# Sliding-window attention and a highway layer: 128-key units in sixteen 32x32 score tiles, v in 512-byte float runs, masks by identity products, a fixed rotation of stages

## The chip, the cores and the metric

The kernel runs on one core of one Trainium2 chip. The metric is the time of one execution on the device in microseconds (us); lower is better. Of the kernel before, three runs gave 235.52, 240.13 and 245.24 us; the median is 240.13. One execution was profiled; the columns and views quoted below are of that one.

The engines are named as in the profile: PE does matrix products (PEld is its loading of the stationary operand), DVE is the vector engine, ACT the scalar engine, POOL the general engine, SP the engine that only issues transfers. DMA queues move data between the chip's main memory and the on-chip memory. Each engine works through its own list of instructions in order, and waits at an instruction until the semaphores that it names are reached.

## The reference

Eight batches, eight heads, 576 positions of 64 numbers each for q, k and v, all float32. Each query sees the 128 keys up to and including its own; a linear penalty by distance, with a slope per head, is added to the scaled scores.

```python
scores = scale * np.matmul(q, k.transpose(0, 1, 3, 2))
rel = pos[:, None] - pos[None, :]
bias = slopes[:, None, None] * (-np.abs(rel).astype(np.float32))[None, :, :]
mask = (rel >= 0) & (rel < window)                # window = 128
scores = np.where(mask, scores + bias[None], -1000000000.0)
attn = softmax(scores)                            # exp, divided by its sum
x = (attn @ v), heads side by side                # 4608 rows of 512
H = np.maximum(x @ w_h, 0.0)
T = 1.0 / (1.0 + np.exp(-(x @ w_t + b_t)))
out = T * H + (1.0 - T) * x
```

So there is an attention part that reads 28 MB of q, k and v, and a highway part with two 512x512 weight matrices for each of 4608 rows.

## The kernel before, in words

The batches are taken two at a time (pair m, 4 of them); r is the batch within a pair. The heads are taken in groups hp of two, hp and hp + 4 (j = 0 and 1), so that one tile of 128 partitions holds 2 batches x 2 heads x 32 groups.

**Loads.** `load` (L103) issues every transfer on POOL's queue, which also turns float32 into bf16 on the way. q and k come as one transfer per pair, hp and tensor (L108), with one run of 18 positions x 64 numbers per partition. v comes as four transfers per pair (L112) straight into its place `VA`, where each partition takes single positions: its runs are 64 numbers, 128 bytes after the conversion. DVE then transposes q and k in 32x32 squares (`tr`, L169), with two bf16 numbers taken as one 32-bit word, so that TR holds a head's numbers along the partitions and its positions along the row.

**Attention.** A unit is (m, s, hp): 128 keys of two batches and two heads. `scores` (L189) multiplies keys by queries on PE with tiles of 32 rows by 64 columns: a quarter of the rows for each (r, j), and the half of the columns that belongs to j. So of the eight squares of 32 rows by 64 columns it uses four. There are 24 products in a unit, each over 192, 128 or 64 queries. ACT takes exp of the result (`soft`, L204) with the penalty's part by key in its bias; DVE multiplies by the window and the rest of the penalty (`mask`, L214). `pv` (L237) multiplies by v with a column of ones appended, in tiles of 64 rows by 128 columns, and `norm` (L249, L251) divides by that column's sum.

**Highway.** For each of 36 blocks of 128 rows: PE transposes x (L260), ACT copies it to the on-chip memory (L265), PE multiplies by w_h (L271) and by w_t (L284), with the bias b_t as a fifth product (L286). ACT takes tanh (L290) and turns it into the gate (L294, 0.5 t + 0.5); DVE does max(., 0) - x (L276) and multiplies by the gate (L298); POOL adds x (L302); SP stores (L309, L313).

**The order of the work** is written by hand in the string ORDER (L15): each letter calls one step (`do`, L315) on the next item of its list in `lists`. What comes from one letter stands in that order on every engine that it touches. The on-chip accumulator memory holds two tiles for scores (`ps_sc`), one for `av` and two `f` tiles that x's transposes and the two products share.

## Time and profile before

| What | Value |
|---|---|
| median of 3 runs | 240.13 us (235.52 to 245.24) |
| profiled execution: its span, first to last instruction (the page gives no other time of it) | 234.4 us |
| PE busy | 148.7 us, 2677 products |
| DVE busy | 141.5 us, 273 instructions |
| ACT busy | 114.4 us, 175 instructions |
| POOL busy | 86.6 us, 95 instructions |
| read from main memory, written to it | 30.41 MB, 9.44 MB |

The page's second part cuts the span into 40 slices of 5.86 us; a digit is the busy share of a slice in tenths. PEclk is the clock that PE was granted, in tenths of full speed. DMA is the mean busy share of the 16 transfer engines, and GB/s what they moved, counted in bytes as written. A row of a list of instructions by line reads: line, engine, operation, output<-inputs, shapes, count | busy time and mean duration in ns of one | idle time before them and what ended it. A row of a timeline reads: start, duration, engine, line, operation, count; several instructions of one form that follow each other are one row. In a timeline the duration of a product runs until its last result is out, so products that follow each other overlap; the start of the next row tells how fast they go in.

### The profile page before, as it was taken

What the parts mean: (1) busy time and instruction counts of PE and PEld (TensorE: products, weight loads), DVE (VectorE), ACT (ScalarE), POOL (GpSimd) and SP (SyncE); (2) the same over time, 40 slices, a digit from 0 to 9 for tenths busy, and PEclk for the clock granted to TensorE, in tenths of its full rate; (3) what the DMA queues carried; (4) which work ended last, traced back from release to release, by engine and by line L of the source; (5) the groups of instructions that cost most, each with busy time, mean ns of one, the idle gap of its engine ahead of it and who ended that gap; (6) DMA issues with size and microseconds to landing.
All of it is one profiled execution on the core that took longest, in us unless ns stands there. A gap on an engine that the chain in (4) does not pass through costs nothing. (4 is left out here: it accounts for less than half of the span.)

```text
span 234.4 us, 6181 instructions
## 1 busy us (share of the span) xinstructions
PE 148.7 (63%) x2677; PEld 88.6 (38%) x2708; DVE 141.5 (60%) x273; ACT 114.4 (49%) x175; POOL 86.6 (37%) x95
## 2 busy tenths in 40 slices
PE   0028122777399303017569869998899999999760
PEld 0017012554244201003236355545556555666320
DVE  2774115885964003010499998999977768796330
ACT  2018100474148600104426765877569589795560
POOL 6192215245411653235924223132233234233331
PEclk9999999999859955555759999999999999999996
DMA  2999999999999999999999941212113221221223
GB/s 25 154 97 74 78 167 184 184 144 135 77 76 133 188 142 71 82 162 207 151 99 218 119 115 48 92 49 78 59 23 116 92 92 65 73 82 60 90 90 91
DMA packets 60380, 25.09 MB, mean 107 GB/s; under 512 B 50625, under 2 KB 51649, under 8 KB 60353
## 3 DMA queue, kind: packets, MB, share of 16 engines
q0 software_dynamic: 55104, 15.26, 153.6%
q1 hardware_dynamic: 5248, 9.44, 12.9%
q8 instruction: 21, 0.34, 0.7%
q14 instruction: 7, 0.05, 0.1%
HBM read 30.41 MB, written 9.44 MB: 170 GB/s over the span
## 5 line engine op out<-in xcount | busy, mean ns | idle before, releaser
L204 ACT ACTIVATE p<-sc,bias 128x768 bf16<-128x768 f32 x64 | 55.7, 907 | 64.5 <-PE sc L189 63.1
L302 POOL TENSOR_TENSOR ot<-uu,x 128x512 f32<-128x512 bf16 x36 | 43.1, 1198 | 75.7 <-DVE uu L298 54.7
L276 DVE SCALAR_TENSOR_TENSOR uu<-f,x 128x512 bf16<-128x512 f32 x36 | 24.6, 685 | 49.4 <-POOL ot L302 40.4
L189 PE MATMUL sc<-tr,tr 32*64 32x192 bf16 (+2 forms) x1152 | 36.6, 267 | 24.7 <-DVE tr L169 16.3
L284 PE MATMUL f<-wT,xt 128*128 128x512 bf16 x128 | 39.9, 413 | 15.2 <-DVE uu L276 12.9
L271 PE MATMUL f<-wH,xt 128*128 128x512 bf16 x129 | 36.3, 390 | 14.8 <-DVE uu L276 13.1
L214 DVE TENSOR_TENSOR p<-p,mk 128x768 bf16<-128x768 bf16 x64 | 37.9, 611 | 9.6 <-ACT p L204 9.6
L290 ACT ACTIVATE tt<-f 128x512 f16<-128x512 f32 x36 | 21.5, 597 | 42.1 <-PE f L286 42.1
L169 DVE STREAM_TRANSPOSE tr<-ld 128x576 uint32<-128x576 uint32 x32 | 39.0, 1243 | 4.2 <-DMA ld<-in_q_dram 4.2
L189 PEld LDWEIGHTS <-tr 32*64 32x64 bf16 x1152 | 27.2, 118 | 29.2 <-DVE tr L169 17.1
L237 PE MATMUL av<-va,p 64*128 64x65 bf16 (+1 forms) x1088 | 26.1, 201 | 19.0 <-DVE x L251 10.7
L237 PEld LDWEIGHTS <-p 64*128 64x128 bf16 (+1 forms) x1088 | 20.9, 102 | 27.5 <-DVE x L251 12.8
L271 PEld LDWEIGHTS <-xt 128*128 128x128 bf16 x144 | 13.0, 99 | 31.9 <-issue 18.9
L251 DVE TENSOR_TENSOR x<-av,rd 128x512 bf16<-128x512 f32 (+1 forms) x32 | 24.3, 758 | 1.2
L284 PEld LDWEIGHTS <-xt 128*128 128x128 bf16 x144 | 13.3, 102 | 30.3 <-issue 19.9
L265 ACT COPY xt<-f 128x512 bf16<-128x512 bf16 x36 | 21.0, 586 | 5.8 <-PE f L260 5.6
L294 ACT ACTIVATE tt<-tt 128x512 f16<-128x512 f16 x36 | 22.9, 636 | 0.6
L112 POOL DMA_DIRECT2D va<-in_v_dram x16 | 18.5, 1168 | 8.5 <-DMA ld<-in_q_dram 8.2
L108 POOL DMA_DIRECT2D ld<-in_q_dram x16 | 11.2, 703 | 24.0 <-DMA va<-in_v_dram 13.2
L298 DVE TENSOR_TENSOR uu<-uu,tt 128x512 bf16<-128x512 bf16 x36 | 15.4, 431 | 7.3 <-ACT tt L294 7.3
L108 POOL DMA_DIRECT2D ld<-in_k_dram x16 | 10.9, 681 | 20.9 <-DMA va<-in_v_dram 14.1
L260 PE MATMUL f<-ident,x 128*128 128x128 bf16 x144 | 14.4, 224 | 4.5 <-DVE uu L276 2.3
(30 smaller groups left out, 46.7 us busy)
## 6 DMA issues: line engine op xcount, KB each, us to landing
out_dram<-ot SPq DMA_DIRECT2D x32, 256.0 KB, 2.0
ld<-in_q_dram POOLq DMA_DIRECT2D x16, 288.0 KB, 19.1
ld<-in_k_dram POOLq DMA_DIRECT2D x16, 288.0 KB, 17.9
va<-in_v_dram POOLq DMA_DIRECT2D x16, 288.0 KB, 17.8
out_dram<-ot SPq DMA_DIRECT2D x8, 128.0 KB, 2.4
wH<-in_moe_w_h_dram POOLq DMA_DIRECT2D x1, 512.0 KB, 20.7
wT<-in_moe_w_t_dram POOLq DMA_DIRECT2D x1, 512.0 KB, 19.1
bT<-in_moe_b_t_dram POOLq DMA_DIRECT2D x1, 1.0 KB, 16.5
```

What stands on the lines that cost most here:

```text
L108: nc.gpsimd.dma_start(out=LD[m % 2, hp, w][:], in_=src)
L169: nc.vector.transpose(out=TR[m % 2, hp, w][:].rearrange("p s e -> p (s e)").bitcast(U32).rearrange("p (s t) -> p t s", t=NT), in_=LD[m % 2 ...
L189: nc.tensor.matmul(out=sc[j * D : (j + 1) * D, r, off : off + n], lhsT=KT[rows, t * D : (t + 1) * D, e], rhs=QT[rows, t * D : t * D + n, e ...
L204: nc.scalar.activation(out=pview(i), in_=SC.pop((m, s, hp))[:, :, 0:384].rearrange("p r (g n) -> p r g n", g=2), func=ACTF.Exp, bias=BIAS[ ...
L214: nc.vector.tensor_tensor(out=p, in0=p, in1=mk.to_broadcast([P, 2, 2, 192]), op=ALU.mult)
L237: nc.tensor.matmul(out=av[orow, j, slot * (D + 1) : (slot + 1) * (D + 1)], lhsT=pt[rows, r, off : off + orow.stop - orow.start], rhs=VA[m] ...
L251: nc.vector.tensor_tensor(out=x[:, :, 0:nt, :], in0=av[:, :, 0:nt, 0:D], in1=rd[:, :, 0:nt, :].to_broadcast([P, 2, nt, D]), op=ALU.mult)
L271: nc.tensor.matmul(out=pa[:], lhsT=XT[m, s, b][:, c, :], rhs=wH[:, c, :], start=c == 0, stop=c == NC - 1)
L276: nc.vector.scalar_tensor_tensor(out=uu[:], in0=PA.pop((m, s, b))[:].rearrange("p (c n) -> p c n", c=NC), scalar=0.0, in1=X[m, s][:, :, b, ...
L284: nc.tensor.matmul(out=pz[:], lhsT=xt[:, c, :], rhs=wT[:, c, :], start=c == 0, stop=False)
L294: nc.scalar.activation(out=tt[:], in_=tt[:], func=ACTF.Copy, bias=0.5, scale=0.5)
L302: nc.gpsimd.tensor_tensor(out=ot[:], in0=UU.pop((m, s, b))[:], in1=X[m, s][:, :, b, :], op=ALU.add)
```

## The change

Every function between the loads and the stores is written anew.

- **Units.** A unit is (b, u): 128 keys of one batch and all eight heads, 40 units in all (the fifth of a batch has 64 keys). The two bits of a head's number of 64 are still taken apart (e), the keys into even and odd positions (t). `scores` uses tiles of 32 rows by 32 columns, all sixteen squares of PE: row quarter j is a head within a half, column quarter kap is 2h + g, with h the half of the heads and g the half of the keys.
- **Masks** are put into the score tile by 16 products per unit of a diagonal (SI, slope / scale) with a table (MT) of minus the distance, or minus a million outside the window. ACT's exp has no bias any more, and DVE's multiplication is gone.
- **v** is loaded by SP's queue as float32 into VS, two positions (512 bytes) to a run, and DVE casts it into VA, four instructions per batch.
- **q and k** come as one transfer per batch and tensor, with the same run length as before; those of the first batch in quarters.
- **Blocks** of 128 rows begin at position 64; the first 64 rows of two batches make one block. `pv` takes 16 products of 64 rows by 128 columns and up to 32 of 32 rows by 64 columns per block. The bias b_t comes as 16 products of 32 rows by 64 columns, put between those.
- **Highway.** The gate's 0.5 t + 0.5 goes from ACT to DVE; the multiplication by the gate goes from DVE to POOL, but for the last two blocks.
- **Order.** ORDER and `lists` are gone. A loop over the 36 blocks issues in each round: the scores of the next block's unit, the product with v of this block, the highway products of the block before, and the transposes of x of this block; the transposes and casts for the next batch and the loads are dealt out in fixed numbers per round. The score tile has one buffer of four banks.

The core of the diff:

```diff
-ORDER = (
-    "LLLLSLLTLTLseTLmLTLsLseLesmLesmLesmLesmLesmLeLmLmLLLLpLnLTpLnTpLsnLeLTpmLTLnsLseLesmLpem"
...
-    return by
+NB, NU, NJ = 8, 5, 4
...
+    LD = {(i, w): cp.tile([P, 2, NT * D], BF16, name=f"ld{i}{w}")
+          for i in range(3) for w in range(2)}
+
+    TR = {(i, w, h): cp.tile([P, S, 2], BF16, name=f"tr{i}{w}{h}")
+          for i in range(2) for w in range(2) for h in range(2)}
+
+    VS = [cp.tile([P, NJ, NU, 2 * D], F32, name=f"vs{i}") for i in range(3)]
+    VA = [cp.tile([P, NJ, NU, 2, D + 1], BF16, name=f"va{i}") for i in range(4)]
+
+    PR = [cp.tile([P, NJ, 384], BF16, name=f"pr{i}") for i in range(6)]
+    PS = [cp.tile([P, NJ, 384], BF16, name=f"ps{i}") for i in range(2)]
...
+    def load_v(b, half, j):
+        rows = 64 * half
+        if j == NJ:
+            nc.sync.dma_start(
+                out=VS[b % 3][rows : rows + 32, :, 4, :],
+                in_=v[b, 4 * half : 4 * half + 4, 512:576].rearrange(
+                    "j (p t) d -> p j (t d)", t=2))
         else:
-            if at[0] < 2:
-                nc.gpsimd.dma_start(
-                    out=(wH, wT)[at[0]][:],
-                    in_=(moe_w_h, moe_w_t)[at[0]].rearrange("(c p) n -> p c n", p=P))
-            else:
-                nc.gpsimd.dma_start(
-                    out=bT[0:1, :], in_=moe_b_t.rearrange("(o n) -> o n", o=1))
+            nc.sync.dma_start(
+                out=VS[b % 3][rows : rows + 64, j, 0:4, :],
+                in_=v[b, 4 * half + j, 0:512].rearrange("(u p t) d -> p u (t d)", p=64, t=2))
+
+    def cast_v(b, j):
+        nc.vector.tensor_copy(
+            out=VA[b % 4][:, j, :, :, 0:D],
+            in_=VS[b % 3][:, j].rearrange("p u (t d) -> p u t d", t=2))
...
+    def scores(b, u):
+        sc = SC[b, u] = ps_sc.tile([P, NJ, 512], F32, name="sc")
+        for h in range(2):
+            for g in range(2):
+                for j in range(NJ):
+                    rows, kap = slice(32 * j, 32 * j + 32), 2 * h + g
+                    o = sc[32 * kap : 32 * kap + 32, j, 0:384]
+                    m = MT[rows, g].rearrange("p t c n -> p (t c n)")
+                    if u == 4:
+                        o = o.rearrange("p (t n) -> p t n", t=2)[:, :, 0:D]
+                        m = MT[rows, g, :, 0, :]
+                    nc.tensor.matmul(out=o, lhsT=SI[rows, h, :], rhs=m, start=True,
+                                     stop=u == 4 and g == 1, tile_position=(32 * j, 32 * kap))
+        parts = [(0, 128 * u, 0, 192 if u < 4 else 64)]
+        if u < 4:
+            parts.append((1, 128 * u + 64, 64, 128))
+        if u < 3:
+            parts.append((1, 128 * u + 192, 0, 64))
+        for t in range(2):
+            for e in range(2):
+                for g, qs, off, n in parts:
+                    for h in range(2):
+                        for j in range(NJ):
+                            rows, kap = slice(32 * j, 32 * j + 32), 2 * h + g
+                            k0 = 128 * u + 64 * g + t
+                            nc.tensor.matmul(
+                                out=sc[32 * kap : 32 * kap + 32, j, 192 * t + off : 192 * t + off + n],
+                                lhsT=TR[b % 2, 1, h][rows, k0 : k0 + 63 : 2, e],
+                                rhs=TR[b % 2, 0, h][rows, qs : qs + n, e],
+                                start=False,
+                                stop=t == 1 and e == 1 and (g, off) in ((0, 0), (1, 0 if u < 3 else 64)),
+                                tile_position=(32 * j, 32 * kap))
...
-    def mask(m, s, hp):
-        p = pview(PT[m, s, hp])
-        mk = MK[:, hp : hp + 1, :].rearrange("p o (g n) -> p o g n", g=2)
-        if s < 3:
-            mk = mk[:, :, 0:1, :]
-        nc.vector.tensor_tensor(out=p, in0=p, in1=mk.to_broadcast([P, 2, 2, 192]), op=ALU.mult)
...
+        nc.scalar.activation(out=o, in_=i, func=ACTF.Exp, scale=scale)
...
+            if tau:
+                for j in range(NJ):
+                    for t in range(2):
+                        for h in range(2):
+                            one_mm(b, tau - 1, slice(64 * h, 64 * h + 64), h, j, t, D, P,
+                                   slice(0, P))
+            ends = []
+            if tau:
+                ends.append((b, tau, 0, D))
+                if tau > 1:
+                    ends.append((b, tau - 2, 1, 0))
+            else:
+                ends += [(b - 1, 0, 0, 0), (b, 0, 0, D)]
+            for j in range(NJ):
+                for t in range(2):
+                    for h in range(2):
+                        for bb, u, g, o in ends:
+                            r = 64 * h + 32 * g
+                            calls.append((bb, u, slice(r, r + 32), h, j, t, 0, D,
+                                          slice(o, o + D)))
+        if zblk is not None:
+            pz = PZ[zblk] = ps_f.tile([P, DM], F32, name="f")
+        for n in range(8):
+            if blk is not None:
+                w = len(calls) // 8
+                for c in calls[n * w : (n + 1) * w]:
+                    one_mm(*c)
+            if zblk is not None:
+                for i in range(2):
+                    nc.tensor.matmul(
+                        out=pz[i * D : (i + 1) * D, n * D : (n + 1) * D],
+                        lhsT=one[32 * i : 32 * i + 32, :],
+                        rhs=bB[32 * i : 32 * i + 32, n * D : (n + 1) * D],
+                        start=n == 0, stop=False, tile_position=(32 * i, i * D))
+
...
+    def to_gate(blk):
+        nc.vector.tensor_scalar(out=TT[blk][:], in0=TT[blk][:], scalar1=0.5, scalar2=0.5,
+                                op0=ALU.mult, op1=ALU.add)
+
+    def gate(blk, eng):
+        eng.tensor_tensor(out=UU[blk][:], in0=UU[blk][:], in1=TT.pop(blk)[:], op=ALU.mult)
+
+    def add_x(blk, eng):
+        ot = OT[blk] = ft.tile([P, DM], F32, name="ot")
+        eng.tensor_tensor(out=ot[:], in0=UU.pop(blk)[:], in1=X.pop(blk)[:], op=ALU.add)
...
-            nc.tensor.matmul(out=pz[:], lhsT=xt[:, c, :], rhs=wT[:, c, :],
-                             start=c == 0, stop=False)
-        nc.tensor.matmul(out=pz[:], lhsT=ones0[:], rhs=bT[:], start=False, stop=True)
...
-    def to_gate(m, s, b):
-        tt = TT[m, s, b]
-        nc.scalar.activation(out=tt[:], in_=tt[:], func=ACTF.Copy, bias=0.5, scale=0.5)
-    def gate(m, s, b):
-        uu = UU[m, s, b][:].rearrange("p c n -> p (c n)")
-        nc.vector.tensor_tensor(out=uu, in0=uu, in1=TT.pop((m, s, b))[:], op=ALU.mult)
-
-    def add_x(m, s, b):
-        ot = OT[m, s, b] = ft.tile([P, NC, P], F32, name="ot")
-        nc.gpsimd.tensor_tensor(out=ot[:], in0=UU.pop((m, s, b))[:], in1=X[m, s][:, :, b, :],
-                                op=ALU.add)
...
-        for n, step in enumerate("".join(ORDER)):
-            if step == "S":
...
-                continue
-            do[step](*by[step][at[step]])
-            at[step] += 1
...
+        load_b(0)
+        load_b(1)
...
+        for part in range(2):
+            for h in range(2):
+                for w in range(2):
+                    tr(0, w, h, part, True)
+                    if part == 0 and h == 0 and w == 0:
+                        v_clear(0)
+                        issue(vloads, 10)
+            if part == 0:
+                scores(0, 0)
+                soft(0, 0)
+        for b in range(1, 3):
+            v_clear(b)
...
+        cst(4, 0)
+        nc.vector.memset(wT[:, :, 0:1], 0.0)
+        load_w(1)
+        load_w(0)
+        scores(0, 1)
+        soft(0, 1)
+        issue(loads, 4)
+        issue(vloads, 10)
...
+        for p in range(N + 1):
+            blk = blocks[p] if p < N else None
+            nxt = blocks[p + 1] if p + 1 < N else None
+            if nxt is not None:
+                scores(*nxt)
+                soft(*nxt)
+            pv(blk, prev)
+
+            tb = -1
+            if blk is not None:
+                tb = blk[0] + (2 if blk[1] == 4 else 1)
+                norm(blk)
+            if p > 2:
+                trn(2 if blk and blk[0] % 2 == 0 and blk[1] in (1, 2) else 1, tb)
+            if prev is not None:
+                mm_z(prev)
+                tanh(prev)
+                to_gate(prev)
+            if nxt is not None and nxt[0] % 2 and nxt[1] == 4 and nxt[0] + 1 < NB:
+                trn(8, nxt[0] + 1)
+                scores(nxt[0] + 1, 0)
+                soft(nxt[0] + 1, 0)
+            if prev is not None:
+                mm_h(prev)
+                relu_sub(prev)
+            if p > 2:
+                trn(1, tb)
+            cst(1, tb)
+            if blk is not None:
+                x_tr(blk)
+                x_copy(blk)
+            if p == 2:
+                trn(8, tb)
+            if prev is not None:
+                last = p >= N - 1
+                gate(prev, nc.vector if last else nc.gpsimd)
+                add_x(prev, nc.vector if last else nc.gpsimd)
+                store(prev)
+            due = max(0, 10 - 2 * (p + 3) * 2 // 9)
+            issue(loads, len(loads) - due if len(loads) > due else 0)
+            due = max(0, 60 - 10 * (p + 3) * 2 // 9)
+            issue(vloads, len(vloads) - due if len(vloads) > due else 0)
+            prev = blk
+        assert not loads and not vloads and not trs and not casts, (loads, vloads, trs, casts)
 
```

The loop moves instructions on every engine. On DVE, in the steady part of the program, names with numbers as the order lists them, a stretch of two units of the kernel before:

```order
L249 RECIPROCAL rd_2335<-av_2291 128x2x4
L251 TENSOR_TENSOR x_2232<-av_2291,rd_2335 128x2x256
L214 TENSOR_TENSOR p5_120<-p5_120,mk_132 128x4x192
L214 TENSOR_TENSOR p6_121<-p6_121,mk_132 128x4x192
L169 STREAM_TRANSPOSE tr130_109<-ld130_93 128x18x32
L169 STREAM_TRANSPOSE tr131_110<-ld131_94 128x18x32
L298 TENSOR_TENSOR uu_2271<-uu_2271,tt_2345 128x512
L214 TENSOR_TENSOR p7_122<-p7_122,mk_132 128x4x192
L276 SCALAR_TENSOR_TENSOR uu_2443<-f_2409,x_1887 128x512
```

and one round of the changed kernel (L280 and L281 divide, L165 transposes q and k, L318 makes the gate, L314 does max(., 0) - x, L101 casts v):

```order
L280 RECIPROCAL rd_3319<-av_3268 128x8
L281 TENSOR_TENSOR x_3318<-av_3268,rd_3319 128x512
L165 STREAM_TRANSPOSE tr001_86<-ld10_81 128x9x32
L318 TENSOR_SCALAR tt_3327<-tt_3327 128x512
L314 SCALAR_TENSOR_TENSOR uu_3335<-f_3330,x_3119 128x512
L165 STREAM_TRANSPOSE tr001_86<-ld10_81 128x9x32
L101 CAST va0_96<-vs1_94 128x10x64
```

The masks (L214) and the multiplication by the gate (L298) are gone from DVE; the gate itself, a cast and two transposes of half the size stand in every round, with the first transpose between the division and the gate.

On POOL, at the start of the program, the kernel before has these transfers behind the first four:

```order
L164 AFFINE_SELECT ident_130<-ident_130 128x128
L112 DMA va0_111<-in_v_dram 64x36x64 x4
L108 DMA ld020_83<-in_q_dram 128x1x1152
L108 DMA ld021_84<-in_k_dram 128x1x1152
L108 DMA ld030_85<-in_q_dram 128x1x1152
L108 DMA ld031_86<-in_k_dram 128x1x1152
L117 DMA wH_127<-in_moe_w_h_dram 128x4x512
L117 DMA wT_128<-in_moe_w_t_dram 128x4x512
```

and the changed kernel these, from the last quarter of the first batch's q and k on:

```order
L83 DMA ld01_80<-in_k_dram 128x1x576
L110 DMA bB_110<-in_moe_b_t_dram 1x16x32 x2
L106 DMA wT_109<-in_moe_w_t_dram 128x4x512
L106 DMA wH_108<-in_moe_w_h_dram 128x4x512
L79 DMA ld10_81<-in_q_dram 128x2x1152
L79 DMA ld11_82<-in_k_dram 128x2x1152
L79 DMA ld20_83<-in_q_dram 128x2x1152
L79 DMA ld21_84<-in_k_dram 128x2x1152
L79 DMA ld00_79<-in_q_dram 128x2x1152
L322 TENSOR_TENSOR uu_762<-uu_762,tt_754 128x512
L326 TENSOR_TENSOR ot_773<-uu_762,x_579 128x512
```

The transfers of v have left POOL's queue; the weights stand before q and k of the second batch, and a write to wT by DVE, behind the four casts of the first batch, must come before the load of wT. On POOL two additions or multiplications per block stand where one stood.

374 lines of the change are left out of this document (174 added, 200 removed).

## Prediction

> **What bounds the kernel now.** First the page's slices, to see whether one thing limits the whole span:
>
> ```profile
> PE   0028122777399303017569869998899999999760
> DVE  2774115885964003010499998999977768796330
> PEclk9999999999859955555759999999999999999996
> DMA  2999999999999999999999941212113221221223
> ```
>
> There are two stages. Up to slice 23 (23 x 5.86 = 135 us) the transfer engines are full and PE mostly idles; then the transfers are nearly idle and PE and DVE are full. The windows give the same in sums (columns: stretch, its length, then busy time and count of PE, PEld, DVE, ACT, POOL; PEclk, DMA share, GB/s):
>
> ```profile
> 0.00:30.00 30.00, 7.25 (x153) 5.50 (x154) 14.45 (x53) 8.46 (x11) 13.27 (x23) 1.00 2.80 86
> 30.00:54.00 24.00, 11.44 (x326) 9.23 (x326) 14.22 (x23) 6.96 (x9) 9.16 (x12) 1.00 1.21 173
> 84.00:110.00 26.00, 7.01 (x29) 2.41 (x30) 2.98 (x6) 2.70 (x4) 9.07 (x12) 0.50 3.32 126
> 136.00:180.00 44.00, 39.28 (x834) 24.24 (x844) 40.06 (x70) 31.53 (x51) 12.73 (x11) 1.00 0.22 74
> 12.00:30.00 18.00, 7.25 (x153) 5.50 (x154) 8.20 (x12) 6.88 (x8) 8.24 (x10) 1.00 4.25 84
> ```
>
> From 12 to 30 us nearly only v is on its way, at 84 GB/s; from 30 to 54 us q, k and the weights, at 173. By bytes, then:
>
> ```profile
> ld<-in_q_dram POOLq DMA_DIRECT2D x16, 288.0 KB, 19.1
> ld<-in_k_dram POOLq DMA_DIRECT2D x16, 288.0 KB, 17.9
> va<-in_v_dram POOLq DMA_DIRECT2D x16, 288.0 KB, 17.8
> wH<-in_moe_w_h_dram POOLq DMA_DIRECT2D x1, 512.0 KB, 20.7
> q0 software_dynamic: 55104, 15.26, 153.6%
> q1 hardware_dynamic: 5248, 9.44, 12.9%
> q8 instruction: 21, 0.34, 0.7%
> ```
>
> q and k are 9.4 MB: 55 us; v is 4.7 MB: 56 us; two weights 6 us. That is 117 us for the first stage. v, a third of the bytes, takes half of it. The second stage has PE at 39.28 of 44 us and DVE at 40.06. So the kernel is 135 us of transfers with some 65 us of PE's work beside them, then some 90 us of PE and DVE, then the tail.
>
> **The change: transfers.** v's runs go from 128 to 512 bytes as written, and their number is halved. No transfer of that form stands in the trace. If a run costs what it did, v takes 28 us; if a byte read costs what it did, 56. I take 40 (5 us per batch), between the ends, since nothing here is nearer to one of them. With q, k and the weights that is 101 us, and the stores add q1's 12.9% of 234.4, 30 us: 131 us, to be spread over the whole span. Transfers stop being the bound, unless they come late at the start.
>
> **PE.** The rows that price it, from the timeline:
>
> ```profile
> 141.63 1.03 PE L284 MATMUL f<-wT,xt 128*128 128x512 bf16 x4
> 142.50 0.38 PE L286 MATMUL f<-bT,ones 128*128 128x512 bf16 x1
> 144.92 0.39 PE L260 MATMUL f<-ident,x 128*128 128x128 bf16 x4
> 145.23 0.87 PE L189 MATMUL sc<-tr,tr 32*64 32x192 bf16 x32
> 146.04 1.09 PE L237 MATMUL av<-va,p 64*128 64x65 bf16 x56
> L237 PE MATMUL av<-va,p 64*128 64x65 bf16 x896 | 22.7, 200 | 19.0 <-DVE x L251 10.7 <-DMA va<-in_v_dram 8.1
> ```
>
> Four products of 512 columns go in during 0.87 us: 2,354 columns per us. The 32 score products have 6,144 columns, 2.61 us one by one; they took 0.87 less the 0.20 that a short product is on its way, so 3.9 ran at once. Four is the number of row quarters, and also of the squares that this layout uses. The 56 products with v took (1.09 - 0.20) / 56 = 16 ns each, two at once.
>
> *Scores* of a full unit: 16 mask products of 384 columns and 96 of 192, 128 and 64. Every one of the sixteen squares gets 384 + 768 = 1,152 columns, 0.49 us if all run at once; with 0.20 on the way and 0.1 to change the tile shape (the transposes should have been in after 0.22, the next row starts after 0.31) 0.79. If only four run at once, as the row has it, 18,432 columns take 2.0 and with the rest 2.3. The fifth unit of a batch has a third: 0.46 or 0.97. Over 32 full and 8 short units and 36 blocks: 0.80 or 2.3 per block. I take 0.80: what ran at once in the row were distinct squares, and they lost nothing by sharing an accumulator bank two by two.
>
> The Trainium skill, "TensorE: Matmul & The Clock Gate", Part 3 on packing small matmuls, reports sixteen 32x32 tiles at 10.6 times the rate of one; by that figure a full unit would take 18,432 / 2,354 / 10.6 + 0.3 = 1.04 us, an estimate 0.25 above mine. No run here shows sixteen yet.
>
> *Products with v*: 16 of the old form, 0.25; 32 small ones and 16 for the bias use single row quarters, 8 ns each if four run at once, 16 if two: 0.38 to 0.76; with 0.3 for way and shape 0.93 to 1.3. I take 1.0, near the row with four at once. *Highway*: 8 x 0.2175 = 1.74; the fifth product is gone. *Transposes of x*: 0.31, as before. Sum per block 0.80 + 1.0 + 1.74 + 0.31 = **3.85 us**.
>
> PE's instructions grow from 5,418 to 12,514, and q8 brings them: 0.7% of 16 x 234.4 is 26 us of one engine's time for 0.34 MB, so 61 us for the new count. That is under a third of the span; I cost it at nothing.
>
> **DVE.**
>
> ```profile
> 161.00 0.41 DVE L298 TENSOR_TENSOR uu<-uu,tt 128x512 bf16<-128x512 bf16 x1
> 161.34 1.25 DVE L169 STREAM_TRANSPOSE tr<-ld 128x576 uint32<-128x576 uint32 x1
> 164.19 2.33 DVE L169 STREAM_TRANSPOSE tr<-ld 128x576 uint32<-128x576 uint32 x2
> 166.37 0.41 DVE L298 TENSOR_TENSOR uu<-uu,tt 128x512 bf16<-128x512 bf16 x1
> 167.16 0.68 DVE L276 SCALAR_TENSOR_TENSOR uu<-f,x 128x512 bf16<-128x512 f32 x1
> 167.76 0.19 DVE L249 RECIPROCAL rd<-av 128x8 f32<-128x8 f32 x1
> 167.98 0.69 DVE L251 TENSOR_TENSOR x<-av,rd 128x512 bf16<-128x512 f32 x1
> 168.59 0.55 DVE L214 TENSOR_TENSOR p<-p,mk 128x768 bf16<-128x768 bf16 x1
> L146 DVE TENSOR_SCALAR mk<-qq,kk 128x512 bf16<-128x512 f32 x1 | 0.5, 480 | 0.0
> L146 DVE TENSOR_SCALAR mk<-qq,kk 128x256 bf16<-128x256 f32 x1 | 0.3, 347 | 0.0
> L214 DVE TENSOR_TENSOR p<-p,mk x64: 530/550/1514, 15.4 to 212.9; 128x768 bf16<-128x768 bf16 x64
> ```
>
> From start to start: division 0.83, max(., 0) - x 0.60. A transpose is 2.18 / 2, its half 0.55; of 64 halves 48 fall on the 33 rounds from the fourth on: 0.80. A cast of 640 numbers isn't in the trace; the two L146 rows (float32 in, bf16 out) give 0.52 ns per number, so 0.55, at twice that slope 0.88; 25 in 33 rounds: 0.42. The gate with one input: nearest is L298 with two, 0.34. Sum **3.0 us**, 0.85 below PE. The masks that go, 64 x 0.55 = 35 us, were beside transfers in one half and on DVE's share of the bound in the other.
>
> **ACT and POOL.**
>
> ```profile
> L204 ACT ACTIVATE p<-sc,bias 128x768 bf16<-128x768 f32 x64 | 55.7, 907 | 64.5 <-PE sc L189 63.1
> L290 ACT ACTIVATE tt<-f 128x512 f16<-128x512 f32 x36 | 21.5, 597 | 42.1 <-PE f L286 42.1
> L265 ACT COPY xt<-f 128x512 bf16<-128x512 bf16 x36 | 21.0, 586 | 5.8 <-PE f L260 5.6
> L302 POOL TENSOR_TENSOR ot<-uu,x x36: 1149/1155/1497, 89.7 to 228.9; 128x512 f32<-128x512 bf16 x36
> ```
>
> Exp over 1,536 numbers: 907 + 768 x (907 - 597) / 256 = 1.84 us at most; (32 x 1.84 + 8 x 0.6) / 36 + 0.60 + 0.59 = 2.95 per round. POOL 2 x 1.155 = 2.3. Both lie beside PE. The one score buffer holds up nothing: exp ends 1.9 us after the scores, and PE has 3.0 of other work between two units.
>
> **The round.** PE issues the scores of the next block, the products with v, w_t, w_h, the transposes of x. The division is done 1 us after the products with v, PE needs it after 1.74; tanh (0.60, after exp) frees its buffer while w_h runs. So PE's own 3.85 sets the round, plus its waits: in 136 to 180 us it was busy 0.89 of the time with DVE as full as itself; with DVE at 3.0 I take 0.92, **4.2 us**.
>
> **The start.**
>
> ```profile
> 1.33 0.89 POOL L108 DMA_DIRECT2D ld<-in_q_dram  x1 [0.81 <-POOLq L340]
> 11.02 3.54 DVE L169 STREAM_TRANSPOSE tr<-ld 128x576 uint32<-128x576 uint32 x3 [0.55 <-DMA ld<-in_q_dram]
> ```
>
> Four loads of 295 kB (1.18 MB, 6.8 us at 173 GB/s) were there at 11.0, so 4.2 us are fixed. The four quarters are half of that: 7.6 us, behind which DVE's tables end near 9.5 (an estimate: the first POOL operation that they need comes behind four issues, as before, and the sixteen operations are of L146's size or less); eight half transposes until 14.5. The loads of v start near 10.7, behind a DVE write, and land near 17; four casts until 19. Only then may wT, wH, q and k of the second batch start: 6 + 6.8 us and 2 us of the third batch's v beside them, so k lands near 34 to 35, and six of its eight half transposes are done at **38**. Until then there is work for three rounds only. From there 33 rounds of 4.2 are 139 us; 1 us for the three rounds with a second unit.
>
> PE idles a few us before 38; from 84 to 110 us, where it was idle three quarters of the time, the granted clock was 0.50, so the first rounds may be slower by a us or two. That is left to the range.
>
> **The tail**: bias and the two products 0.3 + 2 x 0.87 + 0.2 = 2.2, max(., 0) - x 0.7, gate and addition on DVE 1.1, then store and end:
>
> ```profile
> out_dram<-ot SPq DMA_DIRECT2D x32, 256.0 KB, 2.0
> ```
>
> With that landing and the 1 us that the end of a program takes, together 7. Span 38 + 139 + 1 + 7 = **185** against 234.4. The median of the runs is 5.7 above the profiled span; with the same, **191 us**.
>
> **Rivals.**
>
> *Four squares at once.* If a row quarter takes one product at a time, the scores cost 2.3, the small products with v 1.3: 5.65 per block, 6.1 per round with the same waits. 38 + 33 x 6.1 + 8 + 5.7 = 253, slower. It turns to slower (245) at a round of 5.85, which is scores of 2.0 with the small products at 1.3. For it: 3.9 at once in the only row. Against: that layout had only four squares to use.
>
> *DVE and POOL shut each other out.* L214's longest is 1,514 against 530, and L302's 1,497 against 1,149: some pairs met. POOL now has 2.3 us in every round. If every gate and cast on DVE waits out a POOL operation (0.96 each, 1.76 per round), DVE needs 4.7 and the round is 5.1: 38 + 168 + 8 + 5.7 = 220. The Trainium skill, "SBUF — State Buffer", section "Who interferes with whom", says that single-input copies and tensor_scalar in their fast modes and POOL's operations lock each other out for a whole instruction; by that rule the two new DVE operations are the exposed kind, and the long L214 fits it. Against: the gate comes when POOL should be done with the block before.
>
> *v isn't relieved.* Runs cost by bytes: 7 us per batch, and the start, which needs three batches of v beside q and k, ends near 45: 198. The change then doesn't do what it says for v, and still gains, since the first stage is no longer PE's idle time.
>
> **How the numbers follow.** Forecast 0.60 (175 to 208: round 3.85 to 4.6, start 34 to 42). v not relieved 0.12. DVE and POOL 0.12. Four squares 0.10. The rest, 0.06, is several in part, 230 to 245. Range 174 to 230. A measurement of this kernel can tell about 2% from no change. Faster by more: 0.60 + 0.12 + 0.11 + 0.01 = 0.84; within: 0.07; slower: the four squares mostly, 0.09.
>
> **What would show it.** Right: DMA's digits below 9 after some 40 us; PE's at 9 from there to the end, PEclk at full; score rows of some 112 products in under 0.9 us; rounds of 4.2 us; the first products with w_t before 28 us. Wrong: score rows of 2 us or more (four squares); DVE casts or gates above 1 us, with DVE at 9 and PE waiting for division (shut out); DMA at 9 beyond 60 us (v); PE waiting for "issue" in the middle of a row of small products (the supply of instructions).

## The result and the profile after

Five runs of the changed kernel gave 244.67 to 250.32 us, median 247.26; five of the kernel before gave a median of 238.78. Executions of one kernel differ by some per cent, and the ratios here and below compare only those within 1.5% of each kernel's fastest, so they differ a little from the quotients of the medians. The ratio is 1.033, with a 95% interval of 1.023 to 1.044: the change makes the kernel slower, where 191 us was forecast. The profiled execution took 249.96 us, a little over the median; its span is 248.1 us.

The page of the changed kernel, its slices (6.2 us each) and queues:

```profile
PE   0245575667956789588946599766958698596982
DVE  2974127544962389265951269535846299332463
PEclk9999999575979799767997569977988799889998
DMA  3996999991488216972587204991252211202222
q0 software_dynamic: 9152, 10.50, 26.6%
q1 hardware_dynamic: 24960, 18.88, 25.7%
q8 instruction: 49, 0.80, 1.3%
```

The transfers did most of what was forecast. They keep the engines nearly full for nine slices (56 us, where some 40 were forecast) instead of 23, and what remains comes in bursts. But PE, which should have been at 9 from the 40th us on, swings between 4 and 9, and its clock, which was full from the 123rd us to the last slice of the kernel before, dips again and again. q8, which brings the instructions, grew from 21 pieces to 49: 12,514 / 49 and, before, 5,418 / 21 both are about 256 instructions to a piece, and 0.80 MB / 49 is 16 KB.

PE's timeline shows both kinds of round. First one without a stall, from one transposing of x to the next, then the stretch from 157 to 170 us (columns: start, duration, line, operation, count; in brackets the idle time ahead of the row and what ended it), and at the end a row at reduced clock and the first and last transposes of the rounds from the fourth on:

```profile
174.30 0.40 PE L288 MATMUL f<-ident,x 128*128 128x128 bf16 x4
174.63 0.38 PE L184 MATMUL sc<-mt,si 32*32 32x384 bf16 x16
174.80 1.08 PE L198 MATMUL sc<-tr,tr 32*32 32x192 bf16 x96
175.81 0.57 PE L233 MATMUL av<-va,pr 64*128 64x65 bf16 x18
...
176.77 0.81 PE L298 MATMUL f<-wT,xt 128*128 128x512 bf16 x3 [0.16 <-issue]
177.42 1.03 PE L309 MATMUL f<-wH,xt 128*128 128x512 bf16 x4
178.32 0.38 PE L288 MATMUL f<-ident,x 128*128 128x128 bf16 x4
...
157.79 0.28 PE L198 MATMUL sc<-tr,tr 32*32 32x192 bf16 x11
158.77 1.03 PE L198 MATMUL sc<-tr,tr 32*32 32x128 bf16 x85 [0.70 <-issue]
...
163.32 0.18 PE L233 MATMUL av<-va,pr 32*64 32x65 bf16 x1 [2.89 <-issue]
...
170.07 0.30 PE L198 MATMUL sc<-tr,tr 32*32 32x192 bf16 x17 [1.66 <-issue]
...
142.96 1.91 PE L309 MATMUL f<-wH,xt 128*128 128x512 bf16 x4
...
51.05 0.58 PE L288 MATMUL f<-ident,x 128*128 128x128 bf16 x4
239.93 0.38 PE L288 MATMUL f<-ident,x 128*128 128x128 bf16 x4
```

The undisturbed round takes 178.32 - 174.30 = 4.02 us, under the 4.2 that were forecast. But the 32 rounds between the last two rows take 188.88 us, 5.90 each. The difference begins in the middle of rows of small products: 11 score products go in, then PE has nothing for 0.70 us; among the products with v it has nothing for 2.89 us; in the next scores for 1.66 us. No engine and no transfer of data is named, only "issue". A window from the one gap to the next tells how many instructions lie between (columns: stretch, length, busy time and count of PE, PEld, DVE, ACT, POOL; PEclk, DMA share, GB/s); the first two rows are a stretch with stalls at half clock and the undisturbed one behind it:

```profile
133.00:147.00 14.00, 10.44 (x335) 6.16 (x323) 4.52 (x8) 4.77 (x6) 3.46 (x4) 0.51 0.25 67
147.00:158.00 11.00, 10.33 (x362) 6.51 (x360) 10.47 (x21) 6.48 (x9) 6.85 (x6) 1.00 0.50 115
158.60:163.20 4.60, 1.66 (x128) 1.42 (x128) 0.00 (x0) 1.45 (x1) 2.82 (x3) 1.00 0.94 248
163.20:169.90 6.70, 4.92 (x127) 2.63 (x128) 4.10 (x7) 1.18 (x2) 2.22 (x2) 0.75 0.65 134
```

128 products and 128 loads of weights, then 127 and 128 (a record can be missing): PE stops once in every 256 instructions, which is one piece of its list. So it goes on: from the 45th us the trace has 17 stalls of over 0.6 us that end in "issue", and from each to the next lie 127 or 128 products, or a whole multiple of that. The trace also has the packets of q8. In all 17 stalls a piece had landed 1.2 to 1.5 us before PE went on; for the three above it landed at 157.37, 161.98 and 168.57 us. PE's longest waits from the 45th to the 240th us, by sums, and the many short ones ahead of w_t, which stand in undisturbed rounds too (columns: total us, times, longest):

```profile
PE av L233 <- issue: 14.6, 7, 3.0
PE sc L198 <- issue: 13.5, 8, 2.8
PE f L270 <- issue: 3.4, 2, 2.0
PE sc L184 <- issue: 3.0, 1, 3.0
PE f L298 <- issue: 6.6, 32, 0.3
```

The first four are 34.5 us. Against rounds that are all as short as the undisturbed one, the excess is 32 x (5.90 - 4.02) = 60 us. Most of the other 26 us go with the clock, which is 0.51 from 133 to 147 us: four products with w_h take 1.91 us there and 1.03 at full clock. By the trace's record of the clock PE was busy for 45.8 us of the 32 rounds at half clock; at that ratio this is some 21 us more than at full clock, an estimate.

The theory, then: PE's list arrives in pieces of 256 instructions, and the next piece isn't there in time when PE has run through the last one too fast. The rivals: the pieces are late only because they queue behind data on the transfer engines; or, third, the small products are slow for some reason of their own.

### The profile page after: what moved, and what is told of

It reads as the page before. It is cut to its first block, busy times and chain, and to the rows that moved or that the text cites. A ratio compares the mean times of both kernels' runs of the same rounds, so it can differ in the third digit from the quotient of the medians.

```text
span 248.1 us, 13351 instructions
## 1 busy us (share of the span) xinstructions
PE 172.5 (70%) x6218; PEld 108.9 (44%) x6256; DVE 136.8 (55%) x271; ACT 94.6 (38%) x113; POOL 101.7 (41%) x104
## 3 DMA queue, kind: packets, MB, share of 16 engines
q1 hardware_dynamic: 24960, 18.88, 25.7%
## 4 chain that ended last, share of the span: by engine, by line
PE 57%; issue 19%; DVE 10%; DMA 9%; ACT 3%; POOL 2%; SPq 0%; POOLq 0%; ACTq 0%; DVEq 0%
PE f L298 13%; PE f L309 13%; PE sc L198 11%; PE av L233 10%; DMA wH<-in_moe_w_h_dram 5%; PE sc L184 4%; DMA vs<-in_v_dram 4%; DVE tr L165 3%; PE f L288 3%; PE f L270 2%; DVE va L101 2%; DVE uu L314 1%; ACT ps L217 1%; POOL ld L83 1%; ACT tt L303 1%
## 5 line engine op out<-in xcount | busy, mean ns | idle before, releaser
L322 POOL TENSOR_TENSOR uu<-uu,tt 128x512 bf16<-128x512 bf16 x34 | 40.2, 1183 | 122.4 <-DVE uu L314 122.4
L217 ACT ACTIVATE pr<-sc 128x1536 bf16<-128x1536 f32 (+1 forms) x36 | 45.4, 1261 | 43.4 <-PE sc L198 43.3
L198 PE MATMUL sc<-tr,tr 32*32 32x128 bf16 (+2 forms) x3072 | 42.3, 247 | 22.4 <-issue 15.1
L198 PEld LDWEIGHTS <-tr 32*32 32x32 bf16 x3072 | 35.1, 103 | 27.5 <-issue 14.1
L233 PE MATMUL av<-va,pr 32*64 32x65 bf16 (+1 forms) x1344 | 34.4, 212 | 14.0 <-issue 13.8
L165 DVE STREAM_TRANSPOSE tr<-ld 128x288 uint32<-128x288 uint32 x64 | 42.6, 700 | 1.4 <-DMA ld<-in_q_dram 0.7
L298 PE MATMUL f<-wT,xt 128*128 128x512 bf16 x109 | 37.4, 460 | 7.4 <-issue 7.0
L280 DVE RECIPROCAL rd<-av 128x8 f32<-128x8 f32 x36 | 7.3, 203 | 62.9 <-PE av L233 62.9
L314 DVE SCALAR_TENSOR_TENSOR uu<-f,x 128x512 bf16<-128x512 f32 x36 | 24.8, 688 | 16.3 <-PE f L309 16.2
L233 PEld LDWEIGHTS <-pr 32*64 32x64 bf16 (+1 forms) x1344 | 26.5, 113 | 13.8 <-issue 10.1
L101 DVE CAST va<-vs 128x640 bf16<-128x640 f32 x32 | 29.3, 917 | 1.3 <-DMA vs<-in_v_dram 1.3
L270 PE MATMUL f<-bB,one 32*64 32x64 bf16 x576 | 21.9, 210 | 6.8 <-issue 6.0
L281 DVE TENSOR_TENSOR x<-av,rd 128x512 bf16<-128x512 f32 x36 | 24.9, 691 | 1.2
L318 DVE TENSOR_SCALAR tt<-tt 128x512 f16<-128x512 f16 x36 | 10.6, 296 | 19.8 <-ACT tt L303 19.3
```

Source lines behind the costliest of these rows:

```text
L101: nc.vector.tensor_copy(out=VA[b % 4][:, j, :, :, 0:D], in_=VS[b % 3][:, j].rearrange("p u (t d) -> p u t d", t=2))
L165: nc.vector.transpose(out=o, in_=ld[:, h, part * 9 * D : (part + 1) * 9 * D].bitcast(U32).rearrange("p (t i) -> p t i", i=32))
L198: nc.tensor.matmul(out=sc[32 * kap : 32 * kap + 32, j, 192 * t + off : 192 * t + off + n], lhsT=TR[b % 2, 1, h][rows, k0 : k0 + 63 : 2, e] ...
L217: nc.scalar.activation(out=o, in_=i, func=ACTF.Exp, scale=scale)
L233: nc.tensor.matmul(out=av[orow, h, 65 * j : 65 * j + 65], lhsT=PT[bb, u][rows, j, 192 * t + off : 192 * t + off + m], rhs=VA[bb % 4][rows, ...
L270: nc.tensor.matmul(out=pz[i * D : (i + 1) * D, n * D : (n + 1) * D], lhsT=one[32 * i : 32 * i + 32, :], rhs=bB[32 * i : 32 * i + 32, n * D ...
```

## The experiments

### The supply by itself

The edit is a kernel of PE's alone; its core:

```diff
+    def small(n, a):
+        for i in range(n):
+            j, kap = i % 4, i // 4 % 4
+            nc.tensor.matmul(
+                out=a[32 * kap : 32 * kap + 32, j, 0:64], lhsT=ld[32 * j : 32 * j + 32, 0:32],
+                rhs=ld[32 * j : 32 * j + 32, 64:128], start=True, stop=True,
...
+        small(2048, acc[0])
...
+        large(1024, 64, acc[1])
...
+        large(512, 128, acc[0])
...
+        large(512, 192, acc[1])
...
+        small(2048, acc[0])
...
```

> What it is: TensorE alone, five stages one after the other, with nothing else in the first four: 2048 small products (32 rows, 32 columns of weights, 64 columns streamed, the sixteen squares in turn), 1024 products of 128x128 by 64 columns, 512 of 128x128 by 128 columns, 512 by 192 columns, and the 2048 small ones again, this time while SyncE's queue loads v in 512-byte runs. It leaves all of the reference's computation out and stores a constant. Theory 1 (TensorE's instruction list comes in pieces of 256 and a piece takes 2.6 to 3.7 us to come, whatever else is moved): 2048 products and their weight loads are 4096 instructions, 16 pieces, so both stages of small products take 42 to 60 us, with a stall at every 256th instruction, and the one with transfers is no more than a fifth longer; of the large ones, only the products of 64 columns are near the supply's pace. Theory 2 (a piece is late only behind the data on the transfer engines): the first stage of small products runs at the squares' own pace, 2048 of them in under 20 us, with no stall at the 256th instruction, and the last one takes 40 us or more.

Its timeline, three rows of the first stage and two of the last, where v is loaded beside it:

```profile
9.34 1.27 PE L50 MATMUL acc<-ld 32*32 32x64 bf16 x128 [2.04 <-issue]
13.07 1.27 PE L50 MATMUL acc<-ld 32*32 32x64 bf16 x128 [2.46 <-issue]
16.53 1.27 PE L50 MATMUL acc<-ld 32*32 32x64 bf16 x128 [2.19 <-issue]
...
192.69 1.40 PE L50 MATMUL acc<-ld 32*32 32x64 bf16 x128 [2.73 <-issue]
196.42 1.39 PE L50 MATMUL acc<-ld 32*32 32x64 bf16 x128 [2.33 <-issue]
```

and the same kernel's groups by form, for the large products (busy time, mean ns of one, idle time):

```profile
L57 PE MATMUL acc<-ld 128*128 128x64 bf16 x1024 | 31.8, 197 | 0.0
```

The theory of the supply holds in its purest form. With nothing on any other engine and the transfer engines idle, 128 products run in 1.27 us, and then PE stands still for 2.0 to 2.7 us, every time. From piece to piece it is 3.73 and 3.46 us in these rows (13.07 - 9.34, 16.53 - 13.07), and 3.45 to 4.00 over the stage, 3.59 on average. The packets of q8 in the trace show what this time consists of. The transfer of the next piece begins 1.0 to 1.5 us after PE has started on a piece, takes 0.9 to 1.4 us, and PE starts on it 1.2 to 1.5 us after it has landed. With v's transfers beside it, which keep the engines two to three tenths busy, a piece takes 3.67 on average, though the granted clock is 0.5 there: traffic of that size changes little. Products of 128x128 by 64 columns, 31.8 us for 8 pieces of 256 instructions, need 3.97 us a piece and never wait. So a piece of 256 instructions that keeps PE for less than some 3.6 us is paid as 3.6 us.

### v for three batches alone

```diff
-        vloads = [(load_v, b, h, j) for b in range(NB) for j in (4, 0, 1, 2, 3) for h in range(2)]
+        vloads = [(load_v, b, h, j) for b in range(3) for j in (4, 0, 1, 2, 3) for h in range(2)]
...
-            due = max(0, 60 - 10 * (p + 3) * 2 // 9)
+            due = max(0, 10 - 10 * (p + 3) * 2 // 9)
```

> What it is: the changed kernel with v loaded for batches 0 to 2 alone; the casts of the later batches read those again, so v of batches 3 to 7 is left out, and 5.9 of its 9.4 MB in 512-byte runs. TensorE's instructions are the same 12,514. Theory 1 (supply of the list by itself): the stalls at every 256th instruction stay, some 20 of them after 50 us, and the time falls by less than 8 us (over 239 us). Theory 2 (the list is late behind v's 512-byte runs on the transfer engines): the stalls go with the traffic after batch 2's loads, and the time falls towards 200 us.

241.28 us, 6 us less than the changed kernel, and a ratio to the kernel before of 1.029 (1.016 to 1.043). Its slices and a queue from the page, and its waits from the 45th to the 240th us:

```profile
DMA  2996999991367111771177101871121111202222
q1 hardware_dynamic: 12640, 12.98, 17.3%
```

```profile
PE av L233 <- issue: 16.9, 8, 3.4
PE sc L198 <- issue: 14.2, 10, 3.4
```

Half of q1's packets are gone and the stalls are all there. The rival of the traffic falls for this kernel.

### Fewer instructions for the same work

Three kernels take instructions away and leave the columns that PE streams nearly as they are. `wide` makes the second half of a unit's scores one product of 192 columns; `fewer_a` also makes the bias one product of 512 columns; `fewer_b` also makes the masks four products of 64 rows by 128 columns:

```diff
-            parts.append((1, 128 * u + 64, 64, 128))
-        if u < 3:
-            parts.append((1, 128 * u + 192, 0, 64))
+            parts.append((1, 128 * u + 64, 64, 192 if u < 3 else 128))
...
+        nc.tensor.matmul(out=pz[:], lhsT=one[:], rhs=bB[:], start=False, stop=True)
...
-                    nc.tensor.matmul(out=o, lhsT=SI[rows, h, :], rhs=m, start=True,
-                                     stop=u == 4 and g == 1, tile_position=(32 * j, 32 * kap))
+            nc.tensor.matmul(out=o, lhsT=SI[rows, j // 2, :], rhs=m, start=True, stop=False,
+                             skip_group_check=True, tile_position=(64 * (j % 2), 0))
```

> What it is: the changed kernel with only the scores' second half as one product of 192 columns: 10,978 instructions, between the change (12,514, 247 us) and the run with 9,898 (213.5 us). Theory 1: the time follows the number of instructions: (12,514 - 10,978) / (12,514 - 9,898) = 0.59 of the way, 224 to 232 us, unless the bias products, which stand inside the second burst, weigh more than their number.

> What it is: the changed kernel with the same computation in 9,898 instead of 12,514 TensorE instructions: the second half of a unit's scores as one product of 192 columns where the change has one of 128 and one of 64 (so the score tile is 4 x 512 and the exp runs over 2048 instead of 1536 elements), and the bias as one product of 512 columns at the end of z. v's transfers, the 32x32 squares and the masks stay. Columns streamed hardly change. Theory 1 (supply): 21% fewer pieces, so at about 3.6 us a piece at the worst the stalls fall from some 37 us to under 15 and the half clock behind them shortens: 200 to 222 us. Theory 2 (v's traffic): as many bytes in as long runs, so the stalls stay: 240 us or more. Theory 3 (32x32 products are slow by themselves): 240 us or more too, with rounds of the same length.

> What it is: the kernel of the run before (one product of 192 columns, one bias product) with the masks as four products of 64 rows by 128 columns of weights and 512 columns a unit instead of sixteen of 32x32: 8,938 TensorE instructions. The masks' own work is about the same where sixteen squares run at once. Theory 1 (supply): the stalls nearly vanish, 195 to 215 us, below the run before by 3 to 12 us. Theory 2 and theory 3: 240 us or more, as the run before.

| Kernel | PE instructions | Median, us | Kernel before beside it | PE's "issue" waits in scores and products with v, 45th us on |
|---|---|---|---|---|
| changed | 12,514 | 247.26 | 238.78 | 28.1 us, 15 times |
| wide | 10,978 | 225.67 | 239.29 | 17.6 us, 9 times |
| fewer_a | 9,898 | 213.54 | 237.50 | 10.6 us, 8 times |
| fewer_b | 8,938 | 210.79 | 237.50 | 8.6 us, 6 times |

The waits of `fewer_b` from the 45th to the 240th us, and its clock by slices of 5.2 us from the page:

```profile
PE av L228 <- issue: 5.0, 3, 2.4
PE sc L193 <- issue: 3.6, 3, 1.7
```

```profile
PEclk9999999966999799999999999978999999999998
```

The first 1,536 instructions, 6.0 pieces, bring 21.6 us: 3.6 us a piece. That is as much as a piece takes in the supply alone, but the clock rose too (0.91 from the 43rd to the 220th us of `wide`, 0.84 from the 43rd to the 240th of the changed kernel), so the agreement may be luck. The next 4.2 pieces bring 12.1 us, 2.9 each; the last 3.75 only 2.75 us, a little under the 3 to 12 expected: a round of `fewer_b` has about as many instructions as a piece and hardly waits any more. The clock dips in six slices only. `fewer_a` has a ratio of 0.910 (0.892 to 0.927) to the kernel before, `fewer_b` 0.899 (0.887 to 0.912), and the slowest run of the two, 216.84 us, is well under the fastest of the kernel before beside them, 232.85: **the change with fewer instructions beats both kernels.** The squares, v's transfers and the casts are the same in `fewer_a`, and most of what fell is time in which PE has nothing: 46 us from the 43rd to the 240th us of the changed kernel, 22 from the 43rd to the 205th of `fewer_a`. So the third theory falls too.

### The kernel before, with more instructions

```diff
-            for e in range(2):
+            for e, n0 in [(e, n0) for n0 in range(0, n, 64) for e in range(2)]:
...
+                        for c in range(n0, n0 + 64, 64):
+                            nc.tensor.matmul(
+                                out=sc[j * D : (j + 1) * D, r, off + c : off + c + 64],
```

> What it is: the kernel before with nothing of the change, but with each of its score products cut into pieces of 64 columns: the same columns, the same results, 9,258 TensorE instructions instead of 5,418. Theory 1 (the supply of instructions): in the first stage, where TensorE waits for transfers, nothing; in the second, where TensorE sets the time, a unit's scores and products with v bring more than 256 instructions in 2 us, so stalls appear at every 256th, and the kernel before gets 8 to 30 us slower (246 to 268 against 238). Rival (the loss belongs to what is particular to the change, the sixteen squares, the masks as products or the casts): within 2% of the kernel before.

252.52 us (248.18 to 256.89) against 239.29 (234.30 to 244.24): 13 us slower, within the 8 to 30 of the supply theory, but not for the reason it gave. Where it expected nothing, in the stage of the transfers, most of the stalls stand. PE's timeline of this kernel at three of them:

```profile
29.44 1.07 PE L190 MATMUL sc<-tr,tr 32*64 32x64 bf16 x65 [8.59 <-issue]
...
68.09 0.43 PE L190 MATMUL sc<-tr,tr 32*64 32x64 bf16 x17 [7.66 <-issue]
...
134.23 0.31 PE L190 MATMUL sc<-tr,tr 32*64 32x64 bf16 x5 [5.20 <-issue]
```

Its waits over the whole span, then from the 136th us on:

```profile
PE sc L190 <- issue: 40.5, 12, 8.6
...
PE sc L190 <- issue: 3.0, 4, 1.1
```

37.5 of 40.5 us lie before the 136th us, where the transfer engines are full; they are eight stalls of 0.7 to 8.6 us. Where one stall follows another by one piece there, the transfer of the next piece begins 3.7 to 7.4 us after PE has started on the one ahead, by the packets of q8, against 1.0 to 1.5 in the supply alone. So the rival of the traffic, which fell for the changed kernel, is right for a stage whose transfer engines are full. And those stalls weren't hidden, as I had thought: it seems that they put off PE's work of the first stage into the second. How much of the 13 us is theirs isn't shown, since PE is also busy for 155.1 us here and for 148.7 in the kernel before.

The kernel before itself had at least two such stalls, and its timeline has them:

```profile
54.06 0.18 PE L189 MATMUL sc<-tr,tr 32*64 32x64 bf16 x1 [2.97 <-issue]
...
64.47 0.85 PE L189 MATMUL sc<-tr,tr 32*64 32x192 bf16 x14 [3.12 <-issue]
```

3 us in the middle of a row of scores, with nothing named, and 1.6 to 1.7 us before each end a packet of q8 had landed: that PE can wait for a piece could have been read there, and its size from q8's row.

### The same instructions in another order

In the changed kernel (`spread`) and in `fewer_b` (`fewer_c`) the products with w_h are put between the scores and the products with v, so that large ones part the two bursts of small ones:

```diff
+            if prev is not None:
+                mm_h(prev)
+                relu_sub(prev)
             pv(blk, prev)
...
-            if prev is not None:
-                mm_h(prev)
-                relu_sub(prev)
```

> What it is: the changed kernel with the same 12,514 instructions in another order: the four products with w_h of the block before stand between the scores and the products with v, instead of behind w_t. So 0.9 us of large products parts the two bursts of small ones. Theory 1a (a steady pace: 256 instructions per some 3.6 us, whatever their order): a round of 376 instructions needs 5.3 us in any order, so at best 42 + 33 x 5.3 + 8 = 225, and what is gained is under the 22 us between that and 247. Theory 1b (only the burst counts, the supply has enough in hand for a round if the burst is parted): the stalls go, under 215 us. Theory 1a is the one I hold: 230 to 248 us.

> What it is: the fastest version so far (8,938 instructions) with the products with w_h moved between the scores and the products with v. Some 9 us of stalls are left in that version after the 45th us, and its clock is below 0.7 in 3 of 40 slices. Theory 1: a round of some 260 instructions takes 4.3 us, more than the 3.6 of a piece, so parting the bursts takes most of the stalls away: 200 to 210 us. If the supply is no longer its limit: 208 to 213, as before it.

248.48 us for the one, no gain, and just above the 230 to 248 expected; 222.34 for the other, slower than `fewer_b` and outside what was expected. The profiled executions of `fewer_c` and `fewer_b` have spans of 215.9 and 209.5 us. The waits of `fewer_c` over the whole span:

```profile
PE sc L181 <- ACT ps L212: 7.0, 4, 2.0
PE f L297 <- DMA wH<-in_moe_w_h_dram: 6.7, 1, 6.7
...
PE f L297 <- ACT xt L279: 5.7, 10, 1.0
```

The new order lays other waits open. The products with w_h now wait for ACT's copy of x (5.7 us, nothing before), once for w_h's transfer, with the products with v queued behind them (6.7 us, 2.1 before), and the second unit of a round waits longer for ACT's exp of the first (7.0, 4.3 before). That is 13 us, while the stalls in scores and products with v fell by 5.3, to 3.3; together 7.7 us, beside the 6.4 between the two spans. `spread` shows the same trade: from the 43rd to the 240th us its clock is 0.93 and the changed kernel's 0.84, PE is busy for 6 us less and idle for 6 us more. So two things moved at once and this test doesn't tell the two forms of the theory apart; that the count of instructions decides is shown by the runs above.

### The start

The edit is made in `fewer_b`; its core:

```diff
-        issue(loads, 4)
-        issue(vloads, 10)
+        issue(loads, 2)
...
-            cst(1, tb)
+            cst(0 if p < 2 else 2 if p < 4 else 1, tb)
```

> What it is: the fastest version so far (8,938 instructions, 0.90 of the kernel before) with the second batch's v and the third's q and k loaded after the first block's store and addition instead of at the start, and the casts of the second batch's v dealt out two a round in the third and fourth round. Nothing is left out. It tests the step of the prediction that put the end of the start at 38 us: there the first transposes of the second batch's k began at 40.1, behind 4.6 MB of other loads. If those loads beside it are the reason, the transposes of the second batch end some 4 us earlier (by 40 us) and the time falls by 2 to 6 us, to 205 to 209. If the weights and the start's own chain are, nothing moves: 209 to 213. If the later loads then come too late for the fourth to eighth round, it is slower than 213.

225.14 us, against 210.79 for `fewer_b` and 238.07 for the kernel before beside it: the third case (slower than 213), and by more than expected. The timeline of DVE:

```profile
51.05 0.50 DVE L101 CAST va<-vs 128x640 bf16<-128x640 f32 x1 [13.44 <-DMA vs<-in_v_dram]
...
54.67 1.79 DVE L164 STREAM_TRANSPOSE tr<-ld 128x288 uint32<-128x288 uint32 x3
```

k of the second batch landed at 37.0 us instead of 39.2 (its issue at 24.6 and 24.1, landing 12.4 and 15.1 us later): the other loads beside it cost 2 us. But I had put two casts of late v ahead of the transposes on DVE, and they waited until 54 us. So of the start's delay 2 us are the neighbours', and the order that the change has is better than mine.

## Why the prediction was wrong

**The step that failed** is the one on PE's list: "PE's instructions grow from 5,418 to 12,514, and q8 brings them: 0.7% of 16 x 234.4 is 26 us of one engine's time for 0.34 MB, so 61 us for the new count. That is under a third of the span; I cost it at nothing." That is the price to the transfer engine that carries a piece. PE pays another: the time from one piece to the next, 3.45 to 4.00 us and 3.6 on average as the supply alone showed, with nothing else under way. With it the sum reads: from the 43rd us on PE has 11,180 instructions left (1,334 of its rows stand before), 43.7 pieces, at least 157 us at 3.6. In the forecast these were 33 rounds of 4.2, 139 us, so no more than 3.2 us a piece; the supply was the bound even if every piece had been used evenly. It isn't: behind a run of small products PE waits 0.7 to 3.0 us for the next piece, and a piece with the highway in it can't give that time back. The Trainium skill, "Advanced Engine Details and Errata", section "ISA Cache", states a line of 16 KB or 256 instructions and only two lines. The trace agrees with the 256; the time of 3.6 us is in the runs alone.

**The clock** was left to the range as "a us or two" of the first rounds. Beside the stalls it was 0.51 for 14 us at the longest, and some 21 us of the excess go with it, by the estimate above. That stalls cause it is argued from their places and from `fewer_b`, where both shrink; no kernel here held the one and changed the other. `spread` had the better clock and not the better time, with other waits in its place, so how much a full clock would give back stays open.

**The sixteen squares** work at once, as forecast, and the rival of four squares is refuted, though its 253 us lay near the result. A full unit took 175.81 - 174.63 = 1.18 us in the undisturbed round, where I had 0.79; the term was mis-sized. Its 112 products went in at some 10 ns each, and their number counts beside their columns: over the same columns 96 score products took 1.02 us here and 64 took 0.81 in `wide` (medians of the rows at full clock without a stall). The row of 32 that priced the term is two units of the kernel before: 48 of its 64 units have 16 products of 192 columns each, and only the others have 24. The estimate of 1.04 from the Trainium skill, "TensorE: Matmul & The Clock Gate", Part 3, was nearer.

**The other terms of the round** were right: small products with v and bias 0.8 to 0.96 (1.0), highway 1.71 (1.74), transposes 0.33 (0.31); together 4.02 against 3.85, and against 4.2 with the waits.

**v** was right: q1 carried 25.7% of 248.1 us, 63.8, and with v of three batches alone 17.3% of 243.6, 42.1; the difference of 21.6 us for five batches is 35 us for eight, where I took 40 between 28 and 56.

**DVE and POOL** do shut each other out, in one of the two places. From the changed kernel's rows for the tiles that the casts write (least, median and longest duration, first and last start):

```profile
L101 DVE CAST va<-vs x32: 478/1121/1144, 17.7 to 211.7; 128x640 bf16<-128x640 f32 x32
```

Alone a cast takes 0.48 us, under the 0.55 of the forecast; behind POOL's multiplication, where it stands in nearly every round, 1.12. The gate stayed at 0.3. The cost lies beside PE's work, since DVE is busy for 111.5 of the 197 us from the 43rd on.

**The start** ended at 43 to 45 us instead of 38; k of the second batch landed at 40.5 in the changed kernel (issued at 23.8, 16.7 earlier), where I had 34 to 35.

What the prediction listed as wrong signs had the right one among them, PE waiting for "issue" in a row of small products, but no rival with a price stood behind it.

## What to carry to other kernels

Count the instructions of an engine in the stretch that sets the time, and not only their columns: if 256 of them (128 products with their weights) are worked off in under some 3.6 us, they cost 3.6 us, and more where the transfer engines are full. Look for "issue" gaps in the middle of uniform rows, and at the count between them. Small tiles that run at once pay only while each product is long: merging products, even where it computes columns that nobody reads, made 247 us into 211.

## What the runs showed of the hardware

- A piece of PE's list is 256 instructions and 16 KB. From piece to piece it takes 3.45 to 4.00 us with idle transfer engines, 3.59 on average; in `before_split`, where they are full, PE stopped for up to 8.6 us.
- Sixteen squares take small products at one per 8 to 11 ns (128 in 1.27 us with 0.2 on the way, 112 in 1.18 us), so squares of 64 columns, 27 ns each by the 2,354 columns per us of the prediction, keep only about three of sixteen busy.
- A cast of 640 numbers on DVE takes 0.48 us alone and 1.12 beside a POOL operation of 1.16 us; the single-input gate of 512 numbers stayed at 0.3 us.
